# Larger list weights for six scalings and turns in step 34 and 35 of a fused attention and MLP-mixer kernel

## The chip, the cores and the metric

The kernel runs on one core of a Trainium2 chip. The metric is the device time of one execution, in microseconds. All arithmetic is float32.

## The reference

Two blocks follow one another. Attention has 8 batch elements, 12 heads, 448 rows and 64 columns per head; q and k are normalised by their root mean square first:

```python
q_n, k_n = (rmsnorm(q, g_q), rmsnorm(k, g_k))
scores = scale * np.matmul(q_n, k_n.transpose(0, 1, 3, 2))
attn = softmax(scores)                      # over the last axis
x = np.matmul(attn, v)                      # laid out as (8, 448, 768)
```

The mixer then works on each batch element:

```python
xt = x.transpose(0, 2, 1)
h = np.maximum(xt @ w_tok1, 0.0) @ w_tok2   # token mixing, 448 -> 256 -> 448
u = x + h.transpose(0, 2, 1)
h2 = np.maximum(u @ w_ch1, 0.0) @ w_ch2     # channel mixing, 768 -> 1536 -> 768
out = u + h2
```

## The kernel before

The work is cut into *pairs*: a pair is two neighbouring heads of one batch element, so an element has six pairs and there are 48 in all (numbers 0 to 47). While one element is in mixing, attention of the next element is computed beside it. The program is written as lists of items, each a function with a weight in rough microseconds; `merge` takes, again and again, the next item of that list whose share of done weight is the smallest. The result is the order in which instructions are written, and TensorE (PE), VectorE (DVE), ScalarE (ACT) and GpSimd (POOL) keep exactly that order. SyncE (SP), which issues most transfers, is not among the engines whose order is kept: there the framework sorts.

`run` goes through the merged list and adds each weight to a clock. `later(us, fn)` puts work on that clock: the transfers of x through DRAM (`send_x`, `load_x`), and the weight forms of the second channel matrix (`form_items`, lines L308 to L328: loads on SP, sixteen elementwise operations L324 in four parts, three copies and two sends on POOL).

*Attention steps.* For the elements 0 and 1, and up to pair 17, attention is "plain": `att_step(g)` with g = 4 t + s computes a quarter of a pair of pairs (2t, 2t+1). A step's first item is one block of matmuls: scores of two key blocks (L459) and values of two earlier ones (L532); step s = 0 adds the row sums (L512). After it come the step's small items: exponentials' sums (`group_sums`, L500), loads of later pairs (L1514), and preparation of the next two pairs n = 2t+2 and n+1:

- `square` (ACT, L1536), `reduce` (DVE, L1549), and `roots`: `fold` (ACT, L1557), `guess` (DVE, L1566 and L1571) and three Newton steps (L1590 to L1592 on DVE, or L1579 to L1582 on POOL for pair 20 and later);
- `scale` (DVE, L1600) multiplies q and k by the roots; both scalings stand in step s = 2, as the last two entries of `behind`;
- `turn_qk` (DVE transposes L436, then ACT L439 for q) makes the operands of the scores; pair n is turned in step s = 2, pair n+1 in step s = 3. The list is called `turns`. It has two entries for a pair.

q and k of a pair lie in one of two buffers (`qk_t`, even and odd pairs), so the loads of pair n+2 wait for the turns of pair n.

The steps of the change are t = 8 (`t == BIG - 1`), s = 2 and 3: step 34 (pairs 16 and 17; scales pairs 18 and 19, turns pair 18, loads pair 20) and step 35 (turns pair 19, loads pair 21). They are the last plain steps. Pair 18 on is handled by `big_step` in two blocks per pair of pairs; its first block follows step 35.

*What they are merged with.* While steps 26 to 35 run, element 1 is in channel mixing. Its first half is 21 products `ch1` (L1097), three blocks of seven, with weight 2.24 each; its second half is `plain_2` (L1146), twelve halves of weight 4.48, of which six are in this merge and six follow it. A ch1 product is drained from PSUM by DVE or ACT; products with index 4 are copied by ACT (L1119) and added by POOL (L1103, two adds: one makes a piece of the hidden layer, the other the sum r[2] that the product with index 5 needs). Two PSUM buffers `m_ps` alternate between the products.

In front of the merge's result, `x_items` turn the output of attention for element 2 (L837); its two halves are sent to DRAM and loaded back in another layout (L795, L808, L811), the first half on SP and the second on POOL. Token mixing of element 2 begins with L850 and L857, which need those loads.

The lines that build a step's list are the end of `att_step` (L747 to L773); `part(fns, c=0.4)` gives each function of a list the weight c.

Of the kernel before, what the change touches and what calls it, by code (L numbers as in the profile page):

```python
# [83 lines left out]
def whole(ctx, tc, shifted, pre, q, k, v, g_q, g_k, moe_w_tok1, moe_w_tok2, moe_w_ch1, moe_w_ch2, out):  # L84
# [338 lines left out]
    def turn_qk(p, i):  # L423

        qk = st["qk", p]
        if ("qkT", p) not in st:
            st["qkT", p] = pre.qkT[p] if p < len(pre.qkT) else qkT_pool.tile([P, 2, S], F32, name="qkT")[:]
        to = st["qkT", p][:, i, :]
        if pre.plain(p):
            ps = s_tile("t_ps")  # L430
            for c in range(NS):
                o = (i * NS + c) * P
                nc.tensor.transpose(ps[:, c * R:(c + 1) * R], qk[0:R, o:o + P], ident[0:R, 0:R])
            src = ps[:, 0:S]
        else:
            nc.vector.transpose(out=to, in_=qk[:, i * S:(i + 1) * S])  # L436
            src = to
        if i == 0:
            nc.scalar.mul(to, src, g_t[:, 0:1])  # L439
        elif pre.plain(p):  # L440
            nc.scalar.copy(out=to, in_=src)
        if i == 0:
            st.pop(("qk", p))
# [60 lines left out]
    def on_pe(p):  # L504

        return shifted or p < NPAIR
# [39 lines left out]
    def denominators(ps):  # L546

        def begin(p):
            b, j = divmod(p, NPAIR)
            if j == 0:  # L550
                st["uT", b] = uT_pool.tile([P, NC, S], F32, name="uT")
            ps = st.pop(("d", p))

            dt = rd_pool.tile([P, S], F32, name="dt", tag="rd")
            if shifted:
                nc.vector.tensor_scalar(dt[:], ps[:, 0:S], 1e-9, None, ALU.add)
                src = dt[:]
            else:

                src = ps[:, 0:S]  # L560
            nc.vector.transpose(out=dt[:], in_=src)
            st["rc", p] = rc = pre.nt_pool.tile([P, NB], F32, name="rc")
            nc.vector.reciprocal(out=rc[:], in_=dt[:].rearrange("p (n c) -> p n c", c=32)[:, :, 0])

        def raw(p):

            b, j = divmod(p, NPAIR)
            to = st["uT", b][:, j, :]
            nc.scalar.copy(out=to, in_=st["o", p][:, 0:S])
            st["o", p] = to  # L570

        def end(p):
            b, j = divmod(p, NPAIR)
            rd = rd_pool.tile([P, S], F32, name="rd", tag="rd")
            nc.vector.transpose(
                out=rd[:].rearrange("p (n c) -> p n c", c=32),
                in_=st.pop(("rc", p))[:].unsqueeze(2).to_broadcast([P, NB, 32]))
            nc.vector.tensor_tensor(out=st["uT", b][:, j, :], in0=st.pop(("o", p))[:, 0:S], in1=rd[:], op=ALU.mult)

        parts = [lambda p=p: begin(p) for p in ps]  # L580
        if ps[0] < NPAIR:
            parts += [lambda p=p: raw(p) for p in ps]
        return parts + [lambda p=p: end(p) for p in ps]

    NG = 2 * NP
    BIG = NPAIR + NPAIR // 2
# [73 lines left out]
    def att_step(g):  # L660


        t, s = divmod(g, 4)
# [3 lines left out]
        items = []  # L667
# [47 lines left out]
        ahead, sooner, behind, turns = [], [], [], []  # L715
        f = lambda fn, *pairs: [lambda i=i: fn(i, st) for i in pairs]
        scales = lambda n: [lambda i=i: scale(i) for i in (n, n + 1)]
        if g in (1, 2):
            behind = f(pre.square, 3 + g) + f(pre.reduce, 3 + g)
        elif g == 5:  # L720
            ahead, behind = f(pre.square, g // 4 * 2 + 4), f(pre.reduce, g // 4 * 2 + 4)
        elif g == 6:
            ahead, behind = f(pre.square, g // 4 * 2 + 5), f(pre.reduce, g // 4 * 2 + 5)
        elif g in (3, 7):
            behind = pre.roots(g // 4 * 2 + 4, st)
        elif g in (4, 8):
            behind = scales(g // 4 * 2 + 2)
        if live and n < NP:
            late = n < 2 * NPAIR + 2
            if t >= NPAIR // 2 and late:  # L730
                if s == 1:
                    ahead, behind = f(pre.square, n), f(pre.reduce, n) + f(pre.square, n + 1)
                elif s == 2:
                    behind = f(pre.reduce, n + 1) + pre.roots(n, st) + scales(n)
                    if pre.plain(n):
                        sooner, behind = behind[:-2], [lambda: None] * len(behind[:-2]) + behind[-2:]
            elif t >= NPAIR // 2:
                a, b = f(pre.square, n) + f(pre.reduce, n), f(pre.square, n + 1) + f(pre.reduce, n + 1)
                behind = (a, b + pre.roots(n, st), scales(n), [])[s]
            now = {2: [] if pre.plain(n) else [n], 3: [n, n + 1] if pre.plain(n) else [n + 1]}.get(s, [])  # L740
            turns = [lambda q=q, i=i: turn_qk(q, i) for q in now for i in (1, 0)]
# [4 lines left out]
        part = lambda fns, c=0.4: [(c, fn) for fn in fns]  # L746
        if s == 0 and t and not shifted:  # L747
            items += part(denominators((p - 2, p - 1)))
        soon = s == 3 and not inside and not pre.plain(n)
        if soon:  # L750
            items += part(turns)
        if live and not on_pe(p):
            items += [(0.5, lambda k=k: group_sums(t, k)) for k in ((), (1, 2), (3, 4), (5, 6))[s]]

# [10 lines left out]
                  for it in part(pre.loads(j, st, nc.sync, nc.sync), 0.2 if pre.plain(j) else 0.6)]  # L765
        if g == 3:
            items += [it for j in (6, 7) for it in part(pre.loads(j, st, nc.sync, nc.sync), 0.2)]
        items += part(behind)
        if not inside and not soon:
            items += part(turns)  # L770
        if t == BIG - 1 and s > 1 and not shifted:
            items += part(pre.loads(n + s, st, nc.sync, nc.sync), 0.3)
        return items  # L773
# [563 lines left out]

    mixing = set()
    att_items = lambda lo, hi: [it for g in range(lo, hi) for it in att_step(g)]

    run(merge(
        att_items(0, 8) + merge(att_items(8, AHEAD * per + 1), x_items(0, 0)), weight_items(0, BEFORE)))
    left, (some, sums) = [], sum_items()
    for b in range(B):
# [24 lines left out]
        if b + AHEAD < B and (shifted or b < 2):  # L1369
            att = att_items(lo, lo + 10) + x_items(b + AHEAD, 0)  # L1370
            if shifted:
                att += att_items(lo + 10, lo + per)
            elif not b:
                step = att_step(lo + per - 1)
                att += att_items(lo + 10, lo + per - 1) + step[:5] + x_items(1, 1) + step[5:]
            else:
                run(att[:6])
                ahead, block, beside, between = big_step(BIG, False)
                att = att[6:] + att_items(lo + 10, lo + per - 1) + ahead + [block] + beside + between
        elif b + AHEAD < B:  # L1380
            t = (b + AHEAD) * NPAIR // 2
            blocks = [big_step(t + i // 2, i % 2) for i in range(1, NPAIR + 1)]
            blocks[4][3].extend(x_items(b + 1, 0))
            early = place(early, blocks, [near(early, at) for at in BLOCKS], in_seven(b))
# [287 lines left out]
```

## Time and profile before

| | us |
|---|---|
| median of 3 runs | 1268.9 (1266.23 to 1271.95) |
| the profiled execution's own time | 1268.99 |
| its span, first to last instruction | 1267.2 |
| TensorE busy in the span | 1244.7 |
| VectorE busy | 827.8 |
| GpSimd busy | 434.0 |
| ScalarE busy | 397.1 |

How to read it: a line of a group or a timeline names the start, the duration, the engine, the source line, the operation, the tile written and the tiles read, and in brackets the idle time of the engine ahead of it with what ended it. PE is the matmul side of TensorE, PEld its weight loads, SPq the queue of SyncE. A float32 matmul shows as two records. The product of block 1, index 5 is written 1.5 in this text, and "half 0" is the first half of `plain_2`. The stretch that the change sets in order runs from about 270 us (step 25) to about 388 us (half 5), and the work merged into it starts token mixing of element 2 at 414 us. In 378 to 414 us the sixteen DMA engines are busy all the time (share 1.02).

### The profile page before, as it was taken

How to read it: one execution, taken by the hardware profiler on the slowest of the kernel's cores; microseconds unless marked ns; L12 is line 12 of the kernel's file. 1: busy time of each engine (PE TensorE's matmuls, PEld its weight loads, DVE VectorE, ACT ScalarE, POOL GpSimd, SP SyncE). 2: the span in 40 equal slices, each digit the busy share in tenths (PEclk: the TensorE clock that was granted, in tenths of full speed). 3: DMA queues.
4: the chain of work that ended last, by engine and by line, in shares of the span. 5: the costliest groups of instructions: out<-in, count | busy, mean ns of one | idle time of the engine just before them, and what ended most of it. 6: DMA issues, size and time to landing. Idle time of an engine off the chain costs nothing.

```text
span 1267.2 us, 20382 instructions
## 1 busy us (share of the span) xinstructions
PE 1244.7 (98%) x7322; PEld 903.5 (71%) x7322; DVE 827.8 (65%) x1293; ACT 397.1 (31%) x797; POOL 434.0 (34%) x674
## 2 busy tenths in 40 slices
PE   6999999999999999999999999999999999999998
PEld 3444444457745488798778877897787878797998
DVE  6988889756663455867677476766758486554243
ACT  6664433124330134402442143312343034300210
POOL 2311641044994912234224132244122342131222
PEclk9999999999999999999999999999999999999999
DMA  9666696899889786695758757684866865386554
GB/s 210 153 172 178 189 245 177 198 251 261 223 225 265 157 202 157 142 243 110 177 145 209 164 148 179 153 224 108 193 165 144 225 131 153 117 212 144 182 174 105
DMA packets 480274, 228.39 MB, mean 180 GB/s; under 512 B 362900, under 2 KB 440084, under 8 KB 480164
## 3 DMA queue, kind: packets, MB, share of 16 engines
q1 hardware_dynamic: 472626, 211.85, 66.9%
q0 software_dynamic: 4512, 14.46, 4.0%
q8 instruction: 60, 0.98, 0.3%
q10 hardware_dynamic: 3026, 0.69, 0.3%
q14 instruction: 50, 0.41, 0.1%
HBM read 184.26 MB, written 42.66 MB: 179 GB/s over the span
## 4 chain that ended last, share of the span: by engine, by line
PE 86%; DVE 5%; SPq 3%; DMA 2%; issue 1%; ACT 1%; POOL 1%; DVEq 0%; ACTq 0%; POOLq 0%
PE m_ps L1097 26%; PE m_ps L1163 22%; PE s_ps L459 10%; PE o_ps L532 9%; PE m_ps L1067 5%; PE m_ps L977 3%; PE m_ps L850 3%; PE t_ps L850 2%; PE m_ps L1146 1%; PE seven_ps L936 1%; PE d_ps L512 1%; PE m_ps L936 1%; PE m_ps L512 1%; DVE es L500 1%; DMA xs<-xt 1%
## 5 line engine op out<-in xcount | busy, mean ns | idle before, releaser
L1163 PEld LDWEIGHTS m_ps<-hb,unit 128*128 128x128 f32 x1440 | 270.9, 190 | 8.8 <-issue 7.7
L1163 PE MATMUL m_ps<-hb,unit 128*128 128x224 f32 x1440 | 277.2, 354 | 0.0
L1097 PE MATMUL m_ps<-tu,unit 128*128 128x224 f32 x1008 | 201.6, 355 | 1.3 <-ACT r L1107 1.3
L1097 PEld LDWEIGHTS m_ps<-tu,unit 128*128 128x128 f32 x1008 | 189.1, 190 | 15.0 <-issue 9.2
L463 ACT ACTIVATE e<-s_ps 128x448 f32<-128x448 f32 x294 | 138.3, 549 | 149.6 <-PE s_ps L459 148.9
L1097 PE MATMUL m_ps<-uT,unit 128*128 128x224 f32 x756 | 151.2, 354 | 0.6 <-DVE hb L1103 0.6
L1097 PEld LDWEIGHTS m_ps<-uT,unit 128*128 128x128 f32 x756 | 142.2, 190 | 7.7 <-POOL tu L1001 2.8
L459 PE MATMUL s_ps<-qkT 64*64 64x448 f32 x1260 | 144.3, 545 | 0.8 <-ACT x L832 0.8
L532 PE MATMUL o_ps<-e,v 64*64 64x448 f32 x1148 | 130.0, 538 | 0.0
L500 DVE TENSOR_TENSOR es<-es,e 128x896 f32<-128x896 f32 x90 | 102.9, 1143 | 11.0 <-ACT e L463 6.4
L1103 POOL TENSOR_TENSOR hb<-r,r 128x448 f32<-128x448 f32 x21 | 23.8, 1133 | 217.5 <-ACT r L1119 217.5
L1103 DVE TENSOR_TENSOR hb<-m_ps,r 128x448 f32<-128x448 f32 x63 | 39.1, 620 | 88.9 <-POOL r L1103 57.5
L459 PEld LDWEIGHTS s_ps<-qkT 64*64 64x64 f32 x1260 | 45.7, 132 | 67.9 <-issue 56.2
L1579 POOL TENSOR_TENSOR nt<-rs 128x56 f32<-128x56 f32 (+1 forms) x54 | 21.2, 393 | 201.8 <-DVE rs L1571 199.0
L532 PEld LDWEIGHTS o_ps<-e,v 64*64 64x64 f32 x1148 | 46.1, 133 | 61.9 <-issue 59.8
L1178 POOL TENSOR_TENSOR uT<-uT,r 128x448 f32<-128x448 f32 x42 | 51.4, 1241 | 78.2 <-DVE r L1178 46.6
L1104 ACT ACTIVATE hb<-hb 128x448 f32<-128x448 f32 x84 | 48.2, 575 | 90.5 <-DVE hb L1103 68.5
L1549 DVE TENSOR_REDUCE ms<-sq 128x28 f32<-128x896 f32 (+2 forms) x44 | 47.4, 1080 | 43.5 <-ACT sq L1536 36.3
L324 POOL TENSOR_TENSOR raw<-raw 128x128 f32<-128x128 f32 x128 | 65.4, 531 | 20.8 <-DMA raw<-wp 16.3
L1103 DVE TENSOR_TENSOR r<-m_ps,r 128x448 f32<-128x448 f32 x42 | 26.0, 618 | 55.2 <-PE m_ps L1097 55.2
L1174 ACT COPY r<-m_ps 128x448 f32<-128x448 f32 x24 | 12.8, 532 | 156.5 <-PE m_ps L1163 156.5
L1178 DVE TENSOR_TENSOR uT<-uT,m_ps 128x448 f32<-128x448 f32 x41 | 24.9, 619 | 54.8 <-PE m_ps L1163 54.8
(177 smaller groups left out, 1776.1 us busy)
## 6 DMA issues: line engine op xcount, KB each, us to landing
unit<-ws SPq DMA_DIRECT2D x267, 384.0 KB, 4.1
raw<-in_moe_w_ch_dram SPq DMA_DIRECT2D x72, 256.0 KB, 3.6
v<-in_v_dram SPq DMA_DIRECT2D x96, 112.0 KB, 3.6
out_dram<-turned SPq DMA_DIRECT2D x182, 56.0 KB, 2.0
xs<-xt SPq DMA_DIRECT2D x52, 168.0 KB, 4.5
qk_t<-in_q_dram SPq DMA_DIRECT2D x144, 56.0 KB, 3.5
qk_t<-in_k_dram SPq DMA_DIRECT2D x144, 56.0 KB, 3.4
x<-xs SPq DMA_DIRECT2D x39, 192.0 KB, 4.2
```

The source lines that it names most:

```text
L324: nc.gpsimd.tensor_tensor(out=at[o], in0=at[x], in1=at[y], op=ALU.add if op == "+" else ALU.subtract)
L459: nc.tensor.matmul(out=pss[i][rows_of(i, a), 0:S], lhsT=qkT[h, 1, k * D:(k + 1) * D], rhs=qkT[h, 0, :], start=True, stop=True)
L463: nc.scalar.activation(out=e[:, i, :], in_=pss[i][:, 0:S], func=AF.Exp)
L500: nc.vector.tensor_tensor(out=es[:], in0=(es if k > 1 else st["e", t, 0])[:], in1=st["e", t, k][:], op=ALU.add)
L532: nc.tensor.matmul(out=st["o", p][a * D:(a + 1) * D, 0:S], lhsT=vt[rows, k * D:(k + 1) * D], rhs=e[rows, :], **kw)
L850: nc.tensor.matmul(out=st["t1", h][jc][:, 0:HC], lhsT=w1_sb[:, c, jc * P:(jc + 1) * P], rhs=st["x", b, h][:, :, c, :], start=start and c = ...
L1067: nc.tensor.matmul(out=ps, lhsT=a[:, o + 2 * half, :], rhs=natural(half * KF + t) if wide else u[:, half * KC + t, :], start=(t == 0 and h ...
L1097: nc.tensor.matmul(out=ps[:, j * HS:(j + 1) * HS], lhsT=w[:, t, j, :], rhs=m, start=(t == 0), stop=(t == KC - 1))
L1103: add = lambda e, o, x, y: e.tensor_tensor(out=o, in0=x, in1=y, op=ALU.add)
L1104: relu = lambda name: put_off(lambda: nc.scalar.activation(out=h[name], in_=h[name], func=AF.Relu))
L1163: nc.tensor.matmul(out=ps[:, x * HS:(x + 1) * HS], lhsT=st["w"][:, tile_at % 6, :], rhs=hb[:, X_SLOT[f], i, :], start=(i == 0), stop=(i == 3))
L1178: e.tensor_tensor(out=get(out), in0=get(x_), in1=get(y), op=ALU.add if op == "+" else ALU.subtract)
```

## The change

A variable `wide` is 1.3 for steps 34 and 35 of the branch for plain scores, and 0.4 for every other step. The two last entries of `behind` and both entries of `turns` get it as their weight. In step 34 those are scalings 18 and 19 and the two turns of pair 18; in step 35, whose `behind` is empty, the two turns of pair 19. Six items so have a weight of 1.3 instead of 0.4. No instruction is added or taken away.

```diff
         soon = s == 3 and not inside and not pre.plain(n)
+        wide = 1.3 if t == BIG - 1 and s > 1 and not shifted else 0.4
         if soon:
-            items += part(turns)
+            items += part(turns, wide)
...
-        items += part(behind)
+        items += part(behind[:-2]) + part(behind[-2:], wide)
         if not inside and not soon:
-            items += part(turns)
+            items += part(turns, wide)
```

## The prediction

> **What bounds the kernel now.** I read the busy times of the page first, then TensorE's own waits, then the timelines of 262 to 426 us (the stretch that the edited weights set in order), then the chain that ended last in that stretch.
>
> ```profile
> PE 1244.7 (98%) x7322; PEld 903.5 (71%) x7322; DVE 827.8 (65%) x1293; ACT 397.1 (31%) x797; POOL 434.0 (34%) x674
> ```
>
> TensorE (PE) bounds it: 1244.7 of 1267.2 us busy, at a granted clock of 1.000. An edit that moves no matmul out can only change the 22.5 us that are left, 10.0 of them before the first product. TensorE's waits by releaser:
>
> ```profile
> PE first_ps L158 <- DVE ms L1549: 10.0, 1, 10.0
> PE t_ps L857 <- DMA x<-xs: 1.5, 1, 1.5
> PE m_ps L1097 <- ACT r L1107: 1.3, 1, 1.3
> PE m_ps L1097 <- DVE hb L1103: 0.6, 1, 0.6
> ```
>
> The last three lie in the edited stretch. They are all that it has to win: 1.54 + 1.29 + 0.62 = 3.45 us. The second and third come one after the other:
>
> ```profile
> 323.96 2.54 PE L1097 MATMUL m_ps<-uT,unit 128*128 128x224 f32 x12
> 327.12 2.54 PE L1097 MATMUL m_ps<-uT,unit 128*128 128x224 f32 x12 [0.62 <-DVE hb L1103]
> 330.96 2.54 PE L1097 MATMUL m_ps<-tu,unit 128*128 128x224 f32 x12 [1.29 <-ACT r L1107]
> ```
>
> These are channel-mixing products 2.0, 2.1 and 2.2 (block.index in PRODUCTS; twelve records, one product). Two m_ps buffers alternate, so a product waits until the one two before it is drained; 2.1 waits for the add of 1.6, which stands on VectorE (DVE) behind the scalings and turns of pairs 16 and 17. GpSimd (POOL) meanwhile is in one unbroken run from 312.94 on:
>
> ```profile
> 312.94 3.85 POOL L324 TENSOR_TENSOR raw<-raw 128x128 f32<-128x128 f32 x8 [16.31 <-DMA raw<-wp]
> 316.75 1.13 POOL L1103 TENSOR_TENSOR hb<-r,r 128x448 f32<-128x448 f32 x1
> 317.84 1.14 POOL L1103 TENSOR_TENSOR r<-r,r 128x448 f32<-128x448 f32 x1
> 318.93 6.87 POOL L324 TENSOR_TENSOR raw<-raw 128x128 f32<-128x128 f32 x8
> 325.74 0.76 POOL L328 COPY raw<-raw 128x128 f32<-128x128 f32 x3
> 326.56 0.92 POOL L314 DMA_DIRECT2D ws<-raw  x1
> 327.47 0.99 POOL L315 DMA_DIRECT2D ws<-raw  x1
> ```
>
> See that product 1.4's two adds (L1103) stand between the halves of weight form 0 (L324). Last, the chain behind the 1.54 us wait: loads of pair 21, square, reduce, Newton steps, then x of the next element by way of DRAM.
>
> ```profile
> 388.66 3.45 DMA qk_t<-in_k_dram
> 392.34 0.96 ACT sq L1536
> ...
> 402.88 8.55 DMA xs<-xt
> ...
> 414.36 6.03 DMA x<-xs
> 420.39 0.14 issue
> 420.52 1.43 PE t_ps L857 x4
> ```
>
> **The change, part by part.** It adds and removes no instruction. It raises six list weights by 0.9 each: scalings 18, 19 and turns 18 in step 34, turns 19 in step 35. Merging takes next from the list whose (done + half the next item) / total is smaller. The attention list grows from 93.7 to 99.1, the product list stays at 77.92. So two things happen: after the edited items little changes, and everything ahead of them gets a smaller share and moves forward.
>
> *Late part, steps 34 and 35.* Step 34 sits at share 0.726 before and 0.686 after, between plain_2 halves 0 (0.684) and 1 (0.741) both times; step 35 at 0.816 and 0.808, between halves 2 and 3 (0.799, 0.856); the next block at 0.907 and 0.912, between 3 and 4. TensorE's order here does not change at all. On VectorE, two row-sum adds and the two scalings (0.719) now come ahead of half 1's add instead of behind it, and the last row-sum add comes behind half 3's. Half 1 is done at 360.7 and VectorE, busy with Newton steps until 361.25, waits for nothing: same sum, other order, cost 0. The moved row-sum add (1.16 us) would run from half 3's add (373.36 + 0.62) to 375.2; the row-sum matmuls that need it start at 376.31, so its cover is 1.1 us, and if that is gone it costs the difference. Turns 18 keep all their predecessors on VectorE. Cost 0.
>
> *Queue of SyncE (SP).* The order written in the code is kept by PE, DVE, ACT and POOL; SP's is set by the framework, which takes the earliest-written transfer that it believes ready (the trace has form 5's loads at 368.81, ahead of pair 20's at 371.56, though written behind them). In written order, the load of x for the next element (five DMAs, due 12 clock units after its last turn) comes behind pair 21's eight loads before, and ahead of them after. It needs the four xs transfers landed; pair 21's loads need only turns 19, which directly follow on VectorE. So I expect them to bypass it again: 0. If not, it is the rival below. POOL's x load stays ahead of form 6's parts (due 0.6 units later, 6.0 before).
>
> *Early part, steps 28 to 33.* Each moves ahead of one more product: step 28 from 0.205 to 0.194 past product 0.5 (0.197), step 29 past 1.1, step 30 from 0.382 to 0.361 past 1.4 and close behind 1.3, and so on. The six steps take the same TensorE time on either side of a product. What matters is what else passes product 1.4 and 1.3:
>
> 1. Newton steps of pair 16/17 (nine VectorE pieces, 314.44 to 319.87 in the trace, 5.43 us) pass product 1.3's add. That add ran at 313.91; now it comes near 318.5, and product 1.5, which needs its buffer, wants to start at 316.2 (301.2 at the end of product 1.0, plus 2.43 for step 29, three products of 2.4, 3.1 for step 30, 2.4 for 1.4). A wait of about 2.3 us, 0 at least: the same pieces took 2.23 us at 277.20 to 279.43 with POOL idle, which would end it in time. I take 2.3, since POOL is busy in both.
>
> 2. All four parts of form 0 pass product 1.4's adds on POOL. Ahead of them then stand 3.85 + 6.87 + 0.76 + 0.92 + 0.99 = 13.4 us from 312.94: they end at 326.3 + 2.27 = 328.6 instead of 319.0. Product 1.5's add needs that r: VectorE stands at it until 328.6, with turns 17 behind it; ScalarE stands at the relu of the same adds, with the exponentials of step 31 behind it. 1.5's buffer is free at 329.3 and product 2.0 starts there, not at 323.96: +5.3, which contains the 2.3 of point 1. The waits of 0.62 and 1.29 go, as the scalings are then done ahead of 1.5's add: 5.3 - 1.9 = +3.4. Bounds: if the form's loads, now issued one product (2.4 us) sooner, let POOL start that much sooner and the second eight pieces take 3.85 as the first did, r comes 5.4 sooner and 2.0 starts when it did: -1.9. From 2.4 us later, +5.8. I take +2.4: same start less a 1 us gain, as the loads stand in a queue that is issued back to back.
>
> [...]
>
> *Further on.* POOL's later work is an unbroken backlog to 389, so 2.4's adds behind form 2's third quarter end near 347, 1.1 us before half 0 needs that drain. Square 19 now waits on its load with the relu of 2.6 behind it, needed only by the fifth tile of half 1, 3 us in. Both cost 0 under that cover.
>
> *At the end of the stretch* x of the next element lands at 420.4 by a chain of loads, not by TensorE's pace. TensorE reaches it at 418.99, and 2.4 later after the change, which eats the 1.54 us wait. Sum: +2.4 - 1.54 = +0.9 us on the profiled execution's 1268.99 us (span 1267.2 and 1.8 around it), which is 0.1 above the median of 1268.9. Forecast **1270 us**, 0.1% above: no change. Own range 1267 to 1273 (bounds -1.9 and +5.8, less what the wait absorbs).
>
> **Rivals.** *Slower: x's load gets ahead of pair 21's loads on SP.* For it: the written order now says so. Against: it is not ready while xs is in flight (4.5 us median, 8.55 in the chain). Price: xs last issued about 381, landed 385.4, five issues of 2.26 + 1.77, then eight loads in 8.1 us as between 377.49 and 389.14 without the xs pair: the last near 397.5 instead of 389.14, +8.4 us on a chain with no slack: 1277. Each load issued ahead of it takes about 1 us off, so it passes half a percent when six or more of the eight stand behind it.
>
> *A little faster: POOL's form is out of the way.* If r comes in time, 1.29 and 0.62 go and TensorE still waits for x: 1.9 earlier there makes a longer wait, unless the chain also comes earlier because pair 19's loads pass a unit load and form 3's loads (2 us at 346.7 to 348.7). Then all 3.45 us go: 1265.5, within half a percent.
>
> *The change does nothing:* the order near 350 to 380 is as it was on TensorE, and if VectorE and POOL had slack for the early shift too, 1269.
>
> **How the numbers follow.** Half a percent, 6.3 us, is about what a measurement of this kernel tells from no change. Main case 0.55 (1270), the change does nothing 0.08, a little faster 0.15, x's load first 0.17 (two thirds of it above 6.3 us), other orders of SP 0.05, most of them slower. Slower by over half a percent: 0.11 + 0.04 = 0.15. Faster by as much needs 6.3 of the 12.5 us of waits in the whole kernel, and the stretch has 3.45: 0.04. Range 1265 to 1278: from all waits of the stretch gone to the first rival.
>
> **What would show it.** Right: products 2.1 and 2.2 wait for nothing, 1.5 and 2.0 wait 2 to 5 us for VectorE's add, L1103 on POOL stands behind sixteen L324 pieces and two sends; the wait for x in front of L857 shrinks; halves 0 to 3 stand around steps 34 and 35 as before. Wrong: a wait for x of several us with x<-xs ahead of the second run of qk_t issues on SP; a wait in front of the row-sum matmuls near 377; or new waits in later elements, where SP's order may have been rebuilt.

## The result and the profile after

| | before | after |
|---|---|---|
| median, us | 1270.01 (1266.23 to 1272.49) | 1274.95 (1270.22 to 1281.17) |
| ratio of the times, 95% interval | | 1.0041 (1.0025 to 1.0057) |
| the profiled execution's own time | 1268.99 | 1276.11 |
| its span | 1267.2 | 1274.3 |
| granted clock, mean | 1.000 | 0.997 |

The medians are of twelve executions each, so before's is not the 1268.9 of the three shown with its profile. Ratios here and below come with their own intervals and are not the quotients of the medians shown. The medians are 4.9 us apart, and the ratio puts the loss at 0.41%: inside the half percent that I had taken for no change, but its interval lies wholly above 1. The forecast of no change held. Its main value, 1270, did not, and the slower rival, to which I had given a chance of 0.17, came about.

The busy line of the changed kernel's page, which answers to the first line shown of before:

```profile
PE 1251.0 (98%) x7322; PEld 904.8 (71%) x7322; DVE 829.5 (65%) x1293; ACT 396.4 (31%) x797; POOL 434.9 (34%) x674
```

The number of matmuls is the same, but TensorE is busy 6.3 us longer (1251.0 against 1244.7). So most of the 7.1 us of longer span does not show as waiting; some matmuls ran longer. Three places of TensorE's timeline account for it.

**Ahead of the edit.** The written orders of all engines are the same up to step 28, and yet the profiled execution of after is 2.56 us late at step 25 already. The first line of this timeline of TensorE in the changed kernel is from there. The columns are start, duration, engine, line, operation, tiles, count, and in brackets the idle time and its releaser.

```profile
212.26 7.98 PE L1068 MATMUL m_ps<-hb,stage 128*128 128x448 f32 x16 [2.08 <-ACT r L1079]
...
321.69 2.54 PE L1098 MATMUL m_ps<-uT,unit 128*128 128x224 f32 x12 [0.68 <-ACT r L1120]
...
331.20 4.81 PE L1098 MATMUL m_ps<-uT,unit 128*128 128x224 f32 x24 [1.34 <-DVE hb L1104]
...
346.88 2.54 PE L1098 MATMUL m_ps<-uT,unit 128*128 128x224 f32 x12 [0.70 <-ACT r L1120]
...
423.82 0.92 PE L858 MATMUL m_ps<-x,w_sb 64*128 64x384 f32 x4
425.30 0.88 PE L858 MATMUL t_ps<-x,w_sb 64*128 64x384 f32 x2 [0.56 <-ACT h L889]
426.71 0.88 PE L858 MATMUL t_ps<-x,w_sb 64*128 64x384 f32 x2 [0.53 <-DMA x<-xs]
427.52 5.83 PE L851 MATMUL t_ps<-x,w_sb 128*128 128x384 f32 x12
433.18 7.12 PE L978 MATMUL m_ps<-w_sb,h 128*128 128x448 f32 x18
```

A wait of 2.08 us at 212 us and slow records after it (7.98 us; before 6.28) make 3.3 us at 220 us; a wait of 0.65 us that before has at 242 us is missing, and 2.56 is left. It stands where nothing was edited, and of two kernels below whose instructions up to there are the changed kernel's as well, one shows it and the other does not. I take it for a difference between executions, and subtract it where I compare this trace with that of before.

**The early part.** From L750 on, line numbers of the changed kernel are one higher than before's (L1098 was L1097). The next three lines are products 1.5, 2.0 and 2.5. Products 2.1 and 2.2 now wait for nothing (2.1 is the second half of the x24). Products 1.5, 2.0 and 2.5 wait 0.68, 1.34 and 0.70 us instead. The reason for the 1.34 is on GpSimd (the same timeline, of POOL and then of VectorE in the changed kernel):

```profile
314.71 9.14 POOL L324 TENSOR_TENSOR raw<-raw 128x128 f32<-128x128 f32 x16 [16.40 <-issue]
...
327.25 0.99 POOL L315 DMA_DIRECT2D ws<-raw  x1
328.26 1.14 POOL L1104 TENSOR_TENSOR hb<-r,r 128x448 f32<-128x448 f32 x1
329.35 1.14 POOL L1104 TENSOR_TENSOR r<-r,r 128x448 f32<-128x448 f32 x1
```

```profile
330.52 0.62 DVE L1104 TENSOR_TENSOR hb<-m_ps,r 128x448 f32<-128x448 f32 x1 [3.55 <-POOL r L1104]
```

All of form 0, its copies and its sends stand ahead of product 1.4's two adds. The second add ends at 330.49, VectorE's add of 1.5 starts at 330.52 after 3.55 us of idle time, and 2.0 follows. Half 0 of `plain_2` starts at 354.14 against 348.29: +5.85, less 2.56 is +3.3 us.

Ahead of these products stands one more wait, in the values of step 29 (before, then after):

```profile
305.02 0.93 PE L532 MATMUL o_ps<-e,v 64*64 64x448 f32 x8
```

```profile
306.81 1.56 PE L532 MATMUL o_ps<-e,v 64*64 64x448 f32 x4 [0.57 <-DMA v<-in_v_dram]
```

Step 29 comes about 2.3 us sooner, but the two loads of v that it needs are issued when they were (302.11 less 2.56, against 299.43) and land at 306.67 and 307.37. The step's matmuls take 4.54 us, from 303.76 to 308.30, instead of 2.41. Of the kernels below, those with x behind, with the form later and with both have the same wait (4.3 to 5.3 us for the step); in the early half alone and in the last kernel the step takes 2.5 and 2.8 us, and in the kernels with the old order of the early steps 2.4. In this execution the 2.1 us hardly come on top, as far as the trace tells: GpSimd's run up to r is unbroken from 314.71, so without them TensorE would have stood longer for r at product 2.0.

**The late part.** In SP's timeline the loads of pair 21 are the four `qk_t<-in_q_dram` and four `qk_t<-in_k_dram`; `x<-xs` are the five issues of x of element 2, first half. Before:

```profile
376.24 1.15 SPq L795 DMA_DIRECT2D xs<-xt  x2
377.49 2.99 SPq L1514 DMA_DIRECT2D qk_t<-in_q_dram  x1
380.52 3.37 SPq L795 DMA_DIRECT2D xs<-xt  x2
383.93 3.12 SPq L1514 DMA_DIRECT2D qk_t<-in_q_dram  x3
387.10 2.04 SPq L1514 DMA_DIRECT2D qk_t<-in_k_dram  x4
389.19 2.26 SPq L808 DMA_DIRECT2D x<-xs  x3
```

After:

```profile
379.61 8.04 SPq L796 DMA_DIRECT2D xs<-xt  x4
387.74 1.46 SPq L1515 DMA_DIRECT2D qk_t<-in_q_dram  x2
390.14 1.45 SPq L809 DMA_DIRECT2D x<-xs  x3
391.64 2.46 SPq L812 DMA_DIRECT2D x<-xs  x2
394.14 1.86 SPq L1515 DMA_DIRECT2D qk_t<-in_q_dram  x2
396.05 2.13 SPq L1515 DMA_DIRECT2D qk_t<-in_k_dram  x4
```

Two of pair 21's loads bypass x, six stand behind it, and all eight now stand behind the four xs stores as well. The last one is issued by 398.18 instead of 389.14: +9.04, less 2.56 is +6.5 us. The rest of the chain is shorter than before: 28.4 us instead of 31.8, up to the landing of the second of the two loads of x that TensorE waits for. Its end, from the chain of the stretch in the changed kernel (start, duration, what):

```profile
421.87 4.70 DMA x<-xs
426.57 0.14 issue
426.71 0.88 PE t_ps L858 x2
```

That second load lands at 426.57 instead of 420.94, +5.6 us, and the first at 425.16 instead of 420.39. TensorE, itself 5.75 us late in this execution, waits only 0.56 and 0.53 us there. Then comes something that I had no term for: the twelve matmuls L851 take 5.83 us where they took 4.14. The granted clock in stretches of 2 us of the changed kernel (columns: busy time and records of PE, clock, DMA share, GB/s) shows why:

```profile
426.00:428.00 2.00, 1.47 (x5) 0.98 0.87 156
428.00:430.00 2.00, 2.00 (x5) 0.50 0.73 113
430.00:432.00 2.00, 2.00 (x6) 0.66 0.04 4
```

The clock went to 0.50 for 3.41 us (427.93 to 431.34), after the waits were over (in 432 to 434 it is 1.00 again). In the trace of before it is 1.00 in every one of these stretches. At the start of L978 (L977 before), all is settled: 433.18 against 425.86, +7.3 us, as the span has it (+7.1).

### The profile page after: what moved, and what is told of

The parts are those of the page before. It is cut to its first block, busy times and chain, and to the rows that moved or that the text cites. A ratio compares the mean times of both kernels' runs of the same rounds, so it can differ in the third digit from the quotient of the medians.

```text
span 1274.3 us, 20378 instructions
## 1 busy us (share of the span) xinstructions
PE 1251.0 (98%) x7322; PEld 904.8 (71%) x7322; DVE 829.5 (65%) x1293; ACT 396.4 (31%) x797; POOL 434.9 (34%) x674
## 4 chain that ended last, share of the span: by engine, by line
PE 88%; DVE 4%; issue 2%; SPq 2%; POOL 1%; DMA 1%; ACT 1%; DVEq 0%; ACTq 0%; POOLq 0%
PE m_ps L1098 25%; PE m_ps L1164 22%; PE s_ps L459 10%; PE o_ps L532 9%; PE m_ps L1068 5%; PE m_ps L1147 4%; PE m_ps L978 3%; PE m_ps L851 2%; PE t_ps L851 2%; PE seven_ps L937 1%; PE d_ps L512 1%; PE m_ps L937 1%; PE m_ps L512 1%; SPq L1511 1%; SPq L412 1%
## 5 line engine op out<-in xcount | busy, mean ns | idle before, releaser
L1098 PE MATMUL m_ps<-tu,unit 128*128 128x224 f32 x1008 | 201.6, 355 | 0.0
L1098 PEld LDWEIGHTS m_ps<-tu,unit 128*128 128x128 f32 x1008 | 189.1, 190 | 14.1 <-issue 8.5
L1098 PE MATMUL m_ps<-uT,unit 128*128 128x224 f32 x756 | 151.5, 354 | 2.7 <-ACT r L1120 1.4
L1098 PEld LDWEIGHTS m_ps<-uT,unit 128*128 128x128 f32 x756 | 142.1, 190 | 10.5 <-POOL tu L1002 2.8
L324 POOL TENSOR_TENSOR raw<-raw 128x128 f32<-128x128 f32 x128 | 64.8, 526 | 20.9 <-issue 16.4
L1068 PE MATMUL m_ps<-hb,stage 128*128 128x448 f32 x144 | 57.2, 556 | 2.2 <-ACT r L1079 2.1
```

Of the source, the lines that this page charges most:

```text
L324: nc.gpsimd.tensor_tensor(out=at[o], in0=at[x], in1=at[y], op=ALU.add if op == "+" else ALU.subtract)
L1068: nc.tensor.matmul(out=ps, lhsT=a[:, o + 2 * half, :], rhs=natural(half * KF + t) if wide else u[:, half * KC + t, :], start=(t == 0 and h ...
L1098: nc.tensor.matmul(out=ps[:, j * HS:(j + 1) * HS], lhsT=w[:, t, j, :], rhs=m, start=(t == 0), stop=(t == KC - 1))
```

## The experiments

Three theories. **Q, the queue:** x's first load now stands ahead of most of pair 21's loads on SP, and so the chain from those loads to the second half of x ends later; this makes the time. **S, the early shift:** the six steps that moved forward by one product cost TensorE waits around 1.5 to 2.5, and these make it. **F:** within S, the cause is that form 0 stands ahead of 1.4's adds on GpSimd.

For each profiled execution, the place where token mixing of element 2 starts splits into three terms, all against the trace of before. Its values are: first L857 matmul at 418.07, wait for x 1.54, and then sixteen records that take 1.43 + 4.14 = 5.57 us.

| kernel | median, us | ratio (95%) | first L857 comes | waits there | next 16 records | sum | start of L977 | span |
|---|---|---|---|---|---|---|---|---|
| after | 1274.95 | 1.0041 (1.0025 to 1.0057) | +5.75 | -0.45 | +2.02 | +7.3 | +7.3 | +7.1 |
| change's order from step 34 on only | 1276.53 | 1.0060 (1.0047 to 1.0072) | +1.67 | +5.33 | +1.67 | +8.7 | +8.7 | +8.3 |
| change's order up to step 34 only | 1270.05 | 0.9999 (0.9983 to 1.0016) | +4.76 | -1.54 | -0.62 | +2.6 | +2.4 | +2.1 |
| before, x ahead | 1275.26 | 1.0052 (1.0040 to 1.0065) | -0.50 | +4.58 | +2.28 | +6.4 | +6.4 | +6.0 |
| after, x behind | 1270.84 | 1.0013 (1.0001 to 1.0025) | +3.29 | -1.54 | -0.62 | +1.1 | +1.0 | +1.1 |
| after, form later | 1277.60 | 1.0052 (1.0032 to 1.0071) | +3.57 | +4.20 | +1.69 | +9.5 | +9.5 | +9.3 |
| after, form later and x behind | 1272.65 | 1.0027 (1.0011 to 1.0043) | +1.47 | +0.60 | -0.01 | +2.1 | +2.1 | +2.1 |
| before, x last | 1267.59 | 0.9977 (0.9964 to 0.9990) | +0.97 | -1.54 | -0.62 | -1.2 | -1.4 | -1.7 |
| after, form later and x last | 1268.70 | 0.9987 (0.9971 to 1.0002) | +0.19 | -1.54 | -0.52 | -1.9 | -2.0 | -2.4 |

In every row the span differs by what has built up at the start of token mixing, within 0.4 us. What comes later in the kernel is not touched.

**The late half of the change alone, and the early half alone.** The merge is done twice, with the old weights and with the new ones. One kernel takes the old order up to step 34's first item and the new one from there; the other kernel the reverse.

```diff
+    def mixed(att, early):
+        plain = [(0.4 if c == 1.3 else c, fn) for c, fn in att]
+        mark = [fn for c, fn in att if c == 3.2][-2]
+        a, b = merge(plain, early), merge(att, early)
+        head, tail = a, b                 # early half alone: b, a
+        first = [fn for _, fn in head].index(mark)
+        done = {id(fn) for _, fn in head[:first]}
+        return head[:first] + [it for it in tail if id(it[1]) not in done]
...
-        run(merge(att, early) + last)
+        run((mixed(att, early) if b == 1 and not shifted else merge(att, early)) + last)
```

> The kernel before up to step 34 (steps 28 to 33 not moved), the change's order from step 34 on; SP then issues as in the changed kernel: four xs, two loads of pair 21, the five loads of x, the other six loads of pair 21. Theory Q (x's load ahead of pair 21's loads lengthens the chain that ends in x of element 2): 4 to 6 us above the kernel before, about 1275, and TensorE waits 5 us or more in front of L857's second half. Theory S (the early shift of steps 28 to 33 costs TensorE waits at products 1.5, 2.0 and 2.5): no difference from the kernel before, within 1.5 us, and no more than the 1.5 us wait for x.

> The change's order up to step 34 (steps 28 to 33 one product earlier), the order before from step 34 on; pair 21's loads are all ahead of x's load on SP again. Theory S: the waits of the changed kernel around products 1.5, 2.0 and 2.5 stay, 3.3 us more of TensorE by half 0 than before, and the whole difference of about 5 us. Theory Q: the same waits, but the wait for x (1.5 us) takes them up: 0 to 2 us above the kernel before, 1270 to 1272.

The late half alone makes 1276.53 us, the whole loss and a little more; the early half alone makes 1270.05, a ratio of 0.9999. TensorE's timeline in the kernel with the late half (line numbers are ten or eleven higher in these two):

```profile
427.53 2.08 PE L868 MATMUL t_ps<-x,w_sb 64*128 64x384 f32 x4 [6.87 <-DMA x<-xs]
429.53 5.16 PE L861 MATMUL t_ps<-x,w_sb 128*128 128x384 f32 x12
```

and with the early half:

```profile
422.83 0.92 PE L868 MATMUL m_ps<-x,w_sb 64*128 64x384 f32 x4
423.58 0.81 PE L868 MATMUL t_ps<-x,w_sb 64*128 64x384 f32 x4
```

Without the early shift TensorE stands 6.87 us for x. With the early shift alone it has waits of 1.8, 0.7 and 0.7 us near 320 to 347, and the wait for x is gone: x comes no later than it did (its first load lands at 418.87, before 420.39), and TensorE comes after it. So the early part costs what it costs, and the wait for x takes it back. S is not the cause of the loss. This kernel, too, has the 2.2 us wait at 212.

**x ahead, without the change.** Only the due times of x of element 2, first half, are brought forward in the kernel before. (The triple is start of the stores, distance between them, start of the loads, on the clock of the merged list; the entry without a key is (2.0, 2.0, 12.0).)

```diff
-{(1, 1): (2.0, 0.5, 9.0), (2, 1): (0.0, 0.25, 6.0)}
+{(1, 1): (2.0, 0.5, 9.0), (2, 1): (0.0, 0.25, 6.0), (2, 0): (2.0, 0.25, 4.5)}
```

> The kernel before with nothing changed but the clock times of the transfers of x for element 2, first half (step 2.0 to 0.25, load at 4.5 instead of 12.0): SP has the five loads of x ahead of six of pair 21's eight loads, as in the changed kernel; TensorE, VectorE, ScalarE and GpSimd keep the order before. Theory Q: 4 to 6 us slower than before, with the wait in front of L857. Theory S: the same as before within 1.5 us.

SP's order in this kernel became that of after, from weights and orders that are before's otherwise:

```profile
382.46 4.26 SPq L1514 DMA_DIRECT2D qk_t<-in_q_dram  x2
387.50 1.48 SPq L808 DMA_DIRECT2D x<-xs  x3
389.02 2.03 SPq L811 DMA_DIRECT2D x<-xs  x2
391.10 2.12 SPq L1514 DMA_DIRECT2D qk_t<-in_q_dram  x2
393.26 2.10 SPq L1514 DMA_DIRECT2D qk_t<-in_k_dram  x4
```

and TensorE's timeline:

```profile
424.60 2.10 PE L857 MATMUL t_ps<-x,w_sb 64*128 64x384 f32 x4 [6.12 <-DMA x<-xs]
426.64 5.75 PE L850 MATMUL t_ps<-x,w_sb 128*128 128x384 f32 x12
```

1275.26 us, a ratio of 1.0052 against the changed kernel's 1.0041, with nothing of step 28 to 35 moved. The last of pair 21's loads is issued by 395.36 instead of 389.14 (+6.2), and TensorE waits 4.6 us more for x. Q alone makes the size of the loss.

**x behind, in the changed kernel.** The reverse: the entry (2, 0) with a later load puts x behind all of pair 21's loads again.

```diff
-{(1, 1): (2.0, 0.5, 9.0), (2, 1): (0.0, 0.25, 6.0)}
+{(1, 1): (2.0, 0.5, 9.0), (2, 1): (0.0, 0.25, 6.0), (2, 0): (2.0, 2.0, 20.0)}
```

> The changed kernel with x's load for element 2, first half, due at 20.0 instead of 12.0 clock units: on SP all eight loads of pair 21 stand ahead of it again, all else as changed. Theory Q: most of the loss is gone, 0 to 2 us above the kernel before, 1270 to 1272; what is left is TensorE's early waits less the 1.5 us wait for x. Theory S: it stays near 1275.

1270.84 us: of the 0.41% of the change, 0.13% is left. Pair 21's eight loads are issued by 389.87, ahead of x at 389.91, and TensorE goes over the place without a wait:

```profile
421.36 0.92 PE L858 MATMUL m_ps<-x,w_sb 64*128 64x384 f32 x4
422.11 0.81 PE L858 MATMUL t_ps<-x,w_sb 64*128 64x384 f32 x4
```

The rest, 0.13%, is what of the early shift is not taken back any more, +3.29 - 1.54 - 0.62 = +1.1 us in this execution.

**The form later.** `FORMS_FROM` 58.7 instead of 55.0 puts the second half of form 0 behind 1.4's adds on GpSimd again, in the changed kernel; then the same with x behind.

```diff
-FORMS_FROM = 55.0
+FORMS_FROM = 58.7
```

> The changed kernel with all weight forms due 3.7 clock units later (58.7 instead of 55.0), so that product 1.4's two adds stand between the halves of form 0 on POOL again; SP's order of x and pair 21 stays as in the changed kernel. Theory F (the sixteen form pieces ahead of those adds make TensorE wait at product 2.0): that wait, 1.3 us, goes and r of product 1.4 is ready 7 us sooner against the product. Theory Q (the chain to x ends last): the time stays 4 to 6 us above the kernel before, since the chain does not pass there. If it falls by the 1.3 us, the early waits add to the chain.

> The changed kernel with both: forms 3.7 units later, and x's load behind all eight loads of pair 21. With the chain out of the way TensorE's own waits decide: 1 to 2 us below the changed kernel with x behind alone (1270.8), so level with the kernel before, 1269 to 1270. If POOL's form does not matter: 1270.8 again.

With the form later the adds run at 321.14 on GpSimd, between the halves of the form, and product 2.0 follows at 329.12 without a wait. F is right about the cause of that wait. It is not all of the early part: half 0 is still 1.6 us late against step 25, instead of 3.3, as step 29 waits for v (4.48 us). The time does not fall: 1277.60 us, a ratio of 1.0052. TensorE waits for x:

```profile
428.30 2.22 PE L858 MATMUL t_ps<-x,w_sb 64*128 64x384 f32 x4 [5.74 <-DMA x<-xs]
430.45 5.04 PE L851 MATMUL t_ps<-x,w_sb 128*128 128x384 f32 x12
```

With both edits I had expected 1269 to 1270 and got 1272.65. Its timeline has a wait for x again:

```profile
422.59 1.42 PE L858 MATMUL t_ps<-x,w_sb 64*128 64x384 f32 x4 [2.14 <-DMA x<-xs]
```

I had thought of x behind pair 21's loads as the same chain as before. It is not quite: those loads are issued by 392.60 here, as all four xs stores still stand ahead of them, and x lands at 422.45, 2.1 us later than before. TensorE, with a wait less, is too early for it. So the miss is one of my expectation, and it says the same as the run before it: as soon as TensorE is in time, the chain from pair 21's loads to x sets the start of token mixing. The profile explains 2.1 us; its own time was 1271.06, and why the median is 1.6 above that is not shown.

**Pair 21's loads first.** If that chain ends last in the kernel before as well (its 1.54 us wait says so), then all of x, its stores too, put behind pair 21's loads must make before faster. First the kernel before, then the changed one with the form later and x last.

```diff
+(2, 0): (12.0, 0.5, 20.0)      # in the kernel before
+(2, 0): (19.0, 0.5, 27.0)      # in the changed kernel, FORMS_FROM = 58.7
```

> The kernel before with xs for element 2, first half, sent and loaded back behind pair 21's loads (start 12.0, step 0.5, load 20.0): nothing of x stands between pair 20's and pair 21's loads on SP. Theory Q: pair 21's loads end about 5 us sooner, the wait of 1.5 us for x goes, 1 to 2 us below before: 1267.5 to 1269. If the DMA engines are simply full there, x's second half comes no sooner and the time is that of before.

> The changed kernel with forms 3.7 units later and xs for element 2, first half, sent and loaded behind pair 21's loads (start 19.0, step 0.5, load 27.0). If the waits are the three that were named (x, the form's adds on POOL, the scalings ahead of product 1.6's add), none but those at product 2.5 and of 0.6 us at product 1.5 are left: 1266.5 to 1268.5, 1 to 3 us below before.

SP's timeline of the first:

```profile
375.43 1.99 SPq L1514 DMA_DIRECT2D qk_t<-in_q_dram  x4
377.46 2.99 SPq L1514 DMA_DIRECT2D qk_t<-in_k_dram  x4
380.50 5.28 SPq L795 DMA_DIRECT2D xs<-xt  x4
```

and of TensorE:

```profile
419.04 0.92 PE L857 MATMUL m_ps<-x,w_sb 64*128 64x384 f32 x4
419.79 0.81 PE L857 MATMUL t_ps<-x,w_sb 64*128 64x384 f32 x4
```

The loads are through by 380.45, 8.7 us sooner than before, the wait for x is gone, and the time is 1267.59 us, 0.9977 (0.9964 to 0.9990) of before. It is a small gain, but a shown one, and the fastest of these kernels. It cannot be 8.7 us: only the wait for x of 1.54 us and the 0.6 us in the records behind it were there to win. Nor does x come 8.7 us sooner, but 2.5 (417.91 instead of 420.39), because the second half's stores, next on the chain, now wait for VectorE's turns instead (GpSimd's xs at 398.72, after 3.00 us of waiting for xt, only 1.5 sooner than 400.23). In the changed kernel the two repairs bring 1268.70, not told apart from before (0.9971 to 1.0002 holds 1). Its profile has only the 0.7 and 0.7 us waits of products 1.5 and 2.5 left near there.

## Why the prediction was right or wrong

*TensorE bounds the kernel, and only the waits of the stretch are to be won:* right. No experiment left the band of -0.23% to +0.6%.

*Late part on TensorE and VectorE, cost 0:* right. Halves 0 to 3 of `plain_2` stand around steps 34 and 35 as foretold, and the row-sum matmuls near 377 wait for nothing.

*Queue of SP, "So I expect them to bypass it again: 0":* **this is the step that failed.** Two of the eight loads did bypass x, six did not. The argument was that the framework had once put a ready load ahead of a waiting one. One instance of such an order was no ground for a price of 0 on a chain that I had myself shown to have no slack. The rival had it right in kind ("passes half a percent when six or more of the eight stand behind it": it was six: 0.41% in after and 0.52% with x ahead in before, close to that border). It was sized at +8.4 us. The last of the loads came +6.5 later in after and +6.2 with x ahead in before; the two loads that passed account for the difference by the rival's own rate, 1 us each. From there on the rival was wrong too: it carried the loads' lateness to the end in full. With x ahead in before the loads were 6.2 us late, but x landed only 4.1 us later (424.47 against 420.39), and 2.3 us came from the lower clock behind the wait, which had no term. That the loss came near the rival's price is therefore luck in part, and so is the forecast of no change: the mechanism that it stood on, eight loads that bypass x, did not come about.

*Early part, +2.4 us:* point 2 was right in mechanism and size; point 1 was not, and the terms partly made up for each other. Point 1 was a wait of 2.3 us at product 1.5 for 1.3's add. That add ended at 320.99, which is 318.4 without the 2.56 and so as forecast ("near 318.5"), but TensorE came to 1.5 only at 321.0: "The six steps take the same TensorE time on either side of a product" failed for step 29, which took 4.54 us instead of 2.41, waiting for v. The 0.68 us that were left the profile puts to the copy of product 1.4 on ScalarE. The nine Newton pieces took 3.86 us (316.60 to 320.46) and not 5.43. This trace has the pieces between 0.22 and 0.50 us, all beside L324; before has two of 1.06 us beside the adds L1103 (316.75 to 318.98) and the other seven between 0.38 and 0.50. So the old row was too high here, and the measurement decides. Point 2 had r at 328.6 and had product 2.0 start 5.3 later; it was 330.49 - 2.56 = 327.9 and 331.20 - 323.96 - 2.56 = +4.7. The waits of 0.62 and 1.29 went, as said. The 0.70 at product 2.5 was not in the sum. All in all +3.3 for +2.4.

*"which eats the 1.54 us wait":* right where x comes in time. The early half alone shows it: no wait for x, ratio 0.9999. In the change itself there was more than 1.54 to eat, as x came 5.6 us later.

*The sum, 1270 us:* wrong by 4.95 us. What was missing is the late x. Of the +7.3 us of the profiled execution it accounts for 3.7 (-0.45 and +2.02, where a kernel with x in time has -1.54 and -0.62), the wait at 212 us for 2.56, and the early part, less what it takes back, for 1.0. The medians of the changed kernel with and without x behind say 4.1 for the first of these. The range up to 1278 held the median because the rival had set its upper end.

*A little faster:* did not come, and the reason is shown. With r in time (form later) the wait at 2.0 goes, but step 29 still waits for v, and what TensorE gains it stands for x. *The change does nothing:* the early half's 0.9999 is near it, but by two shifts that cancel.

What stays open: single executions of the changed kernel lie between 1270.22 and 1281.17, while those with the late half alone lie between 1275.71 and 1277.28. A profile of one of the low ones was not had. The granted clock drops in some of them and not in others: it is 0.999 to 1.000 in the six below 1274 us and 0.995 to 0.997 in five of the six above 1276. Why it does, and how much the early waits vary, is not shown.

## What to carry to other kernels

When weights of a merged list are changed, look at every queue whose order the list only suggests: here the TensorE order was foreseen instruction by instruction, and the loss came from five transfers that slipped in front of six others on SP; a step that was moved forward past the landing of its own load of v cost up to 2.9 us of TensorE besides. Follow the chain that ends last back to its first load, and ask what may come ahead of that load; a wait of 1.5 us at its end says that time added ahead of it is paid, if not in full (6.2 us on the loads became 4.1 us on x). Then try the cheap reverse: moving the due time of one transfer took the loss away, and moving it farther made the kernel before faster as well.

## What the runs showed of the hardware

A wait of TensorE cost more than its length. In the three kernels in which it stood 5.74 to 6.87 us for x, the next sixteen records took 7.24 to 7.85 us instead of the 4.95 that they take without a wait. The stretches of the kernel with x ahead in before show the clock (columns as above):

```profile
422.00:424.00 2.00, 0.00 (x0) 0.77 1.13 271
424.00:426.00 2.00, 1.40 (x4) 0.50 1.09 169
...
428.00:430.00 2.00, 2.00 (x5) 0.52 0.00 0
430.00:432.00 2.00, 2.00 (x8) 1.00 0.91 258
```

The clock falls to 0.50 while TensorE still waits, some 4.6 us after its last matmul (418.48), and is back at 1.00 some 5.3 us after the next one. With the late half alone it falls some 4.1 us after the last matmul (420.66) and is back some 4.1 us after the next one; with form later it is 2.9 us (422.56 to 425.47) and some 4.0 us. In all three it is at 0.50 for some 6.8 us. In after the record of the clock has 0.50 twice inside the kernel, for 3.41 us each time (from 212.89 and from 427.93), and the 211.63 us at 1.00 between the two are about 62 times as long. Shorter waits did not always bring the lower clock: in after, one of 2.08 us (near 212) and two of 0.56 and 0.53 us (near 426) were followed by 0.50 for 3.41 us, while a wait of 1.54 in before and one of 2.14 with form later and x behind were followed by 1.00. So the length of a wait does not decide alone, and no run here shows what else does.
